# A recurrent attention, a soft and a hard mixture of experts in one launch: the last region's loads, gate logits, constants and order

## Chip, cores and metric

One Trainium2 core runs the whole program as one launch. The metric is device time in microseconds; the kernel before was run three times (median 297.85, from 297.54 to 299.38). All times below are counted from the start of one profiled execution of the kernel before.

## The reference

Three layers in a row, float32, 3072 tokens of 384 features:

1. A gated linear recurrence (4 batches, 8 heads, 768 steps, 48 x 48 states): `S = a*S + k v^T`, `y = q S`, with a complex decay `a`.
2. A soft mixture of experts: `logits = x @ phi` (32 slots, 8 experts of 4); a softmax over tokens mixes the tokens into slots, each expert is `relu(slot @ w1[e]) @ w2[e]` (384 to 1024 to 384), and a softmax over the slots, row by row, mixes slot outputs into tokens.
3. A hard mixture: `logits = x @ w_gate` (8 experts), `e = argmax(logits)`, and each token's output is `gate * (relu(x @ w1[e]) @ w2[e])`, where `gate` is the softmax value of the chosen expert.

The kernel uses that the tokens after layer 2 are mixtures `c @ slot_out` of 32 slots that lie close together. It guesses one expert for all tokens from the mean slot, computes layer 3 for that expert alone, and checks at the end, with flags, that the guess holds for every token; a slow general path stands behind an If.

## The kernel before

`build` writes out three regions, each a list of operations (`Sched`: engine, estimated time, what it reads and writes) and a fixed order for that list, which is stored as an encoded string (`ORDER[0]` to `ORDER[2]`) and applied by `follow`. Each engine executes its own operations in that order; engines wait for one another by semaphores. Where the planner's estimate leaves TensorE a gap, `emit` puts small filler matmuls into the third region (`fill(7)`, line L695; two of them here).

Region 1 (0 to 227 us) is the recurrence. Region 2 (227.6 to 253 us) is layer 2's experts. TensorE streams the weights past 32-column stationary operands (first products L765, second products L794, transposes L774 between them) without a gap. VectorE meanwhile makes the row softmax `cc` from the logits (L847 to L853), its deviation from 1/32 (L880 to L883, which ends in one number per token; TensorE turns it at L885 and broadcasts it at L889), and a threefold copy `c4` of `cc` in the weight buffer `wl[2]` (L860). The region ends with the slot outputs `so4` (L809, ScalarE) and the guessed expert's number `ei` (L822, VectorE).

Region 3 (253 us to the end) is layer 3:

- The mixing weights are turned: for m = 0 to 5, four transposes (L871), a copy to `cS` on ScalarE (L874), and on VectorE a subtraction that replaces one of the three copies by its rounding remainder (L875).
- The gate logits: `so4 @ w_gate` (L898) gives `W2S`, 96 x 8 (split in two by L841 and L842); 24 matmuls with `cS` as the stationary operand and 8 moving columns each (L908) give the logits with tokens on partitions. VectorE takes the maximum (L913) and from it the exponents, the gate and the chosen expert (L914 to L919, L927 to L930); the two matmuls L922 and L925 turn the largest and the smallest choice for the flags.
- The guessed expert's weights: SyncE reads `ei` into a register (L947), then issues two DMAs for the first layer (`m1`, `wl[0]`, 768 KB each, L950) and five for the second (`m2`, `wl[1]`, 384 or 192 KB each, L958). Pieces of `m2` are split into a rounded part `m2h` (L962, ScalarE) and a remainder `m2l` (L964).
- The hidden layer at slot level, in two halves of 512 units: L992 (24 matmuls of 32 x 128), a copy `Gs` (L399) and a square `sq` (L996), transposes by L999 and sums by L1000. VectorE finds the units whose sign is not the same for all tokens (`mixed`, L1006) and numbers them by small matmuls (L1012 to L1016); units that are positive for all tokens (`pos`) enter a linear product, the mixed ones (at most 96) a selection matrix `Pm` (L1021, L1025).
- TensorE accumulates, in one bank, the second layer for the linear and the selected units: `lo` (L1052), `hi` (L1056), `ml` (L1060), two matmuls of 384 columns per piece each, and two float32 products L1044; `Gm` (L1034) collects the selected units' first layer. Results are `W` (split in two, L399 and L1071) and `GmS`.
- The output stage: six products of `GmS` with `cS` (L1079), relu and its remainder (L1080, L1082), and per token tile three matmuls with `W` (L1089, L1090, L1093), scaled by `gate` (L1101, L1102) and written out by 14 DMAs (L1104).

Small constants are made on VectorE at the start of region 3: `okc` (L1110 to L1112, which feed the flag product L1114), unit rows in `GmS` (L983), `trib` and `oneb` (L970, L971), a zero matrix `zr` and zeros in `Pm` (L980, L981).

Of the kernel before, what the change touches and what calls it, by code (L numbers as in the profile page):

```python
# [76 lines left out]
    "6aWAK1ONyC$N<a$&;Zl`*Z|xB-~i+R3;+-S7yu*yTma|*>;N19Gyw1bDF7@0^Z-NvIRHEW_yGI>K>#2CYye~cF#t&bOaM>-XaH~kbO3n(SO9zg2muTM5CIecQ~-<s7y)1akN|)HgaC*DlmM9kpa7%*"  # L77
    "oB*f*tN;K31Oc=FxB$EWzyQPmumBwa",
    "5Ca$h8~_Xhr~n89tN;`P^Z)<=3;+ZG5CH4|@BrWd<N!zj7z0cI=m0DOBmgJ?Gy^aIGyos~2mm|)KmbqxQ~<C5zyK5gEC4tFSO8oAU;tzQ`~Uy}L;z?22mu5EYyc1ebO0Cu3;`SgJOLyD6almVm;fvR"
    "_y9lwNC6-LGyy~bOaUkX!~ie>I04K6Pyx6AlmS!$SOHuCWC6$km;ulLU;&5$XaSr7i~(!`Z~=S)fB|&@paF0I*Z_C|gaOq6qyfDEyaB)gtO2M2+yIaPumQ9I90Pa&oB(_Ppa6sbGy;GCI066y1OmhX"  # L80
    ")Bzv^$N{(k*a6@HqyXFj%mL8><N^2r>;XIiPy+M;2m<i|=>hx!R03E6XaZ~kKmuI?NCI#I6apCnMFLC$3<A&s)B+F!WC9!lAp#@<C<1f>c>>r1d;)<2oC2T%qymfrU;>Z=gaU~I<N_=L=>psWFan4G"
    "i~uA9lmeIn;R2`v`~t87v;wRG$O4c6^a7LsC<E*QFa!7k@dCI4y#fRS00Y1RI0MB3%mM",
# [202 lines left out]
def build(tc, a):  # L285
# [69 lines left out]
    def dma(nbytes, fn, w=(), r=()):  # L355
        op("SP", max(480, nbytes / 340), fn, r=r, w=w, lat=2000)
# [365 lines left out]
    def dma(nbytes, fn, w=(), r=()):  # L722
        op("SP", max(480, nbytes / 360), fn, r=r, w=w, lat=2000)
# [98 lines left out]
    V(8, lambda: vec.tensor_reduce(out=ei[:, 0:1], in_=sp[:, :8], axis=AX.X, op=ALU.max), ["sp"], ["ei"])  # L822
# [8 lines left out]
    W2S = t2("W2S", [128, NE], F32R)  # L831
# [60 lines left out]
    def decl_gate():  # L892
# [6 lines left out]

        M(650, f, ["so4"], [kb_g, "W2S"], kb_g)  # L900

        split(kb_g, W2S, NE, "W2S")
        kb_l = s.bank()

        for m in range(6):
            def f(m=m):
                for u in range(4 * m, 4 * m + 4):
                    pe.matmul(bank(kb_l)[:, NE * u:NE * u + NE], cS[:96, 128 * u:128 * u + 128], W2S[:96], start=True, stop=True)  # L908

            M(430, f, ["W2S", ("cS", m)] + ([kb_l] if m else []), [kb_l] + ([] if m else ["lg"]), None if m else kb_l)  # L910
        lv = lambda: bank(kb_l)[:, :NU * NE].rearrange("p (u e) -> p u e", e=NE)
        b8 = lambda t: t[:, :, None].to_broadcast([128, NU, NE])
        V(192, lambda: vec.tensor_reduce(out=gm, in_=lv(), axis=AX.X, op=ALU.max), [kb_l], ["gm"])  # L913
        V(192, lambda: vec.tensor_tensor(out=eq, in0=lv(), in1=b8(gm), op=ALU.is_equal), [kb_l, "gm"], ["eq"])  # L914
        V(192, lambda: vec.tensor_tensor(out=lg, in0=lv(), in1=b8(gm), op=ALU.subtract), [kb_l, "gm"], ["lg"])
# [11 lines left out]
        A(192, lambda: act(out=lg, in_=lg, func=AF.Exp), ["lg"], ["lg"])  # L927
        V(192, lambda: vec.tensor_reduce(out=gate, in_=lg, axis=AX.X, op=ALU.add), ["lg"], ["gate"])
        V(24, lambda: vec.tensor_scalar(out=gate, in0=gate, scalar1=1e-9, scalar2=None, op0=ALU.add), ["gate"], ["gate"])
        V(200, lambda: vec.reciprocal(out=gate, in_=gate), ["gate"], ["gate"])  # L930

# [14 lines left out]
    m2 = wl[1].rearrange("p (k f) -> p k f", k=8)  # L946
    idx = nc.sync.value_load(ei[0:1, 0:1], min_val=0, max_val=NE)  # L947
    op("SP", 850, lambda: None, w=[("m1", 0)])
    for i in range(2):
        dma(786432, lambda i=i: nc.sync.dma_start(out=m1[:, :, 512 * i:512 * i + 512], in_=a["m2w1"][bass.ds(idx, 1), :, 512 * i:512 * i + 512].rearrange("o (k p) f -> p (o k) f", p=128)),  # L950
            w=[("m1", i)])
# [17 lines left out]
    mixed, trib, oneb = (tf(n, [128, k], BF16) for n, k in (("mixed", 8), ("trib", 128), ("oneb", 128)))  # L969
    V(128, lambda: vec.tensor_copy(out=trib, in_=tri), [], ["trib"], True)  # L970
    V(128, lambda: vec.tensor_copy(out=oneb, in_=ones), [], ["oneb"], True)  # L971
# [4 lines left out]
    GmS = tf("GmS", [96, 128], F32R)  # L976
    W = [tf(f"W{i}", [128, DM], F32R) for i in range(2)]
    zr = tf("zr", [128, 128], F32R)
    kb_gm, kb_a = s.bank(), s.bank()
    V(128, lambda: (vec.tensor_scalar(out=zr, in0=tri, scalar1=0.0, scalar2=None, op0=ALU.mult),  # L980
                    vec.tensor_scalar(out=Pm[:, :, 128:128 + NM], in0=tri[:, None, :NM].to_broadcast([128, 8, NM]), scalar1=0.0, scalar2=None, op0=ALU.mult)), [], ["zr"], True)  # L981
# [391 lines left out]
```

## Time and profile before

| what | value |
|---|---|
| median of three runs | 297.85 us |
| the profiled execution, and its span | 298.1 us, 296.3 us |
| TensorE busy over the span | 275.4 us (93%) |
| region 3 up to the first output matmul | 253.0 to 274.2 us |
| output stage | 274.2 to 288.7 us |
| granted TensorE clock, mean of the span | 0.979 |

Times are microseconds from the start of the execution. A busy TensorE is not TensorE at its peak, since its matmuls are pipelined. The granted clock is a share of 2.4 GHz: 1.00 is 2.4 GHz and 0.50 is 1.2 GHz. A chain of waits lists, in order of time, the pieces of work each of which released the next, back from the last instruction. The 1.8 us between time and span lie outside the recorded instructions.

### The profile page before, as it was taken

Reading aid. Unit: us, or ns where it says so; the run is one execution under the profiler, and the core shown is the slowest. Engines: PE = TensorE matmul, PEld = TensorE weight load, DVE = VectorE, ACT = ScalarE, POOL = GpSimd, SP = SyncE. Lnnn points to the kernel's source line nnn. Section 1 sums busy time; section 2 is a strip of 40 time slices with the busy share of each in tenths; the row PEclk is TensorE's granted clock in tenths of the full one; section 3 lists DMA queues with packets and bytes.
Section 4 is the critical chain, followed back from the end, with each engine's and each line's share of the span. In section 5 each row is a group of like instructions: output and inputs, shape, how many; then the busy total and the mean of one; then the engine's idle time right before and its main releaser. Section 6 shows DMA issues by size and latency. Waiting matters only on the chain.

```text
span 296.3 us, 7880 instructions
## 1 busy us (share of the span) xinstructions
PE 275.4 (93%) x3156; PEld 224.2 (76%) x3156; DVE 239.5 (81%) x493; ACT 228.0 (77%) x429; POOL 117.8 (40%) x81
## 2 busy tenths in 40 slices
PE   0799999999999899999999999999999999899990
PEld 0567688788987798979789898998985344788970
DVE  2579999999999999999999998989647722758850
ACT  3869999999999899999999999987354211525760
POOL 0005657566666756576666736662100000000000
PEclk9999999999999999999999999999999999959996
DMA  6645989834996544342434230199876692380593
GB/s 221 208 135 212 382 297 323 324 80 164 297 376 225 199 137 162 124 143 65 150 88 157 59 105 25 42 329 306 292 263 215 194 376 73 108 319 0 213 327 113
DMA packets 27709, 57.98 MB, mean 196 GB/s; under 512 B 1824, under 2 KB 17568, under 8 KB 27664
## 3 DMA queue, kind: packets, MB, share of 16 engines
q1 hardware_dynamic: 27664, 57.39, 56.4%
q8 instruction: 27, 0.44, 0.6%
q14 instruction: 18, 0.15, 0.2%
HBM read 52.66 MB, written 4.72 MB: 194 GB/s over the span
## 4 chain that ended last, share of the span: by engine, by line
PE 66%; DVE 20%; ACT 6%; issue 3%; DMA 2%; POOL 0%; SPq 0%; POOLq 0%; DVEq 0%
PE bank L526 10%; PE bank L516 10%; PE bank L539 6%; PE bank L543 4%; PE bank L765 4%; PE bank L794 4%; PE bank L457 3%; PE bank L551 3%; PE bank L695 3%; DVE sc L532 2%; PE bank L582 2%; DMA reim<-reim 2%; ACT L697 2%; PE bank L452 2%; PE bank L1089 2%
## 5 line engine op out<-in xcount | busy, mean ns | idle before, releaser
L506 POOL TENSOR_TENSOR kqp<-kqi,lt 128x768 f32<-128x768 f32 x46 | 83.3, 1826 | 59.5 <-ACT lt L427 18.4
L516 PE MATMUL bank<-cst,kqp 128*112 128x128 f32 x384 | 54.0, 276 | 0.0
L526 PE MATMUL bank<-qT,kT 112*128 112x128 f32 x384 | 51.3, 280 | 1.0 <-ACT kT L399 0.4
L526 PEld LDWEIGHTS bank<-qT,kT 112*128 112x128 f32 x384 | 46.4, 191 | 3.5 <-ACT kT L399 1.0
L516 PEld LDWEIGHTS bank<-cst,kqp 128*112 128x112 f32 x384 | 42.0, 133 | 5.8 <-issue 2.2
L697 ACT ACT_TABLE_LOAD x29 | 37.2, 1283 | 1.2 <-PEq L1356 0.7
L539 PE MATMUL bank<-sc,v 128*48 128x128 f32 x384 | 36.8, 277 | 0.0
L532 DVE TENSOR_TENSOR sc<-bank,cst 128x512 f32<-128x512 f32 x48 | 32.8, 686 | 3.1 <-PE bank L526 2.4
L543 PE MATMUL bank<-qT,St 112*48 112x128 f32 x320 | 31.1, 272 | 0.0
L539 PEld LDWEIGHTS bank<-sc,v 128*48 128x48 f32 x384 | 20.2, 122 | 5.9 <-issue 4.2
L419 POOL TENSOR_TENSOR lt<-reim,lt 128x768 f32<-128x768 f32 (+1 forms) x10 | 17.5, 1746 | 12.4 <-ACT lt L418 3.8
L551 PEld LDWEIGHTS bank<-v,kqp 128*48 128x48 f32 x640 | 17.7, 124 | 4.6 <-issue 2.7
L399 ACT COPY qT<-bank 112x512 f32<-112x512 f32 x35 | 20.6, 592 | 0.4 <-PE bank L516 0.4
L695 PE MATMUL bank<-cst 128*48 128x128 f32 x82 | 12.7, 315 | 8.7 <-DMA cst<-cst 8.7
L448 POOL TENSOR_TENSOR hl<-lt,hl 128x384 fp32r<-128x384 f32 x15 | 15.3, 1017 | 13.8 <-ACT hl L446 3.1
L551 PE MATMUL bank<-v,kqp 128*48 128x48 f32 x640 | 20.3, 210 | 0.0
L399 ACT COPY kT<-bank 112x512 f32<-112x512 f32 x30 | 17.2, 587 | 3.6 <-PE bank L516 3.5
L695 PEld LDWEIGHTS bank<-cst 128*48 128x48 f32 x82 | 10.4, 143 | 12.3 <-issue 12.1
L543 PEld LDWEIGHTS bank<-qT,St 112*48 112x48 f32 x320 | 19.1, 123 | 0.0
L399 ACT COPY yT<-bank 112x512 f32<-112x512 f32 x18 | 10.6, 588 | 6.6 <-PE bank L543 6.6
L860 POOL COPY wl<-cc 128x384 f32<-128x384 f32 x1 | 0.7, 659 | 36.3 <-PE bank L794 36.3
L452 PE MATMUL bank<-hl,trir 128*128 128x384 f32 x34 | 14.5, 428 | 0.4 <-DVE acc L651 0.4
(249 smaller groups left out, 626.9 us busy)
## 6 DMA issues: line engine op xcount, KB each, us to landing
wr<-w SPq DMA_DIRECT2D x8, 1536.0 KB, 9.1
kqi<-kq SPq DMA_DIRECT2D x24, 384.0 KB, 3.3
reim<-reim SPq DMA_DIRECT2D x11, 768.0 KB, 4.6
wl<-w SPq DMA_DIRECT2D x5, 1536.0 KB, 7.8
v<-v SPq DMA_DIRECT2D x24, 192.0 KB, 3.7
wr<-w SPq DMA_DIRECT2D x6, 768.0 KB, 8.5
out<-osb SPq DMA_DIRECT2D x10, 384.0 KB, 2.7
wl<-m2w SPq DMA_DIRECT2D x2, 768.0 KB, 5.3
```

The source lines that it names most:

```text
L399: v = {"A": ("ACT", t_act(n, True), lambda: nc.scalar.copy(out=out, in_=in_()), False), "D": ("DVE", t_dve(n), lambda: vec.tensor_copy(out ...
L419: either("P", n, lambda e: e.tensor_tensor(out=l1, in0=im, in1=l0, op=ALU.mult), r=[kim] + k0, w=k1)
L452: pe.matmul(o(), trir, hl[:, 0], start=True, stop=False)
L506: either(e, 768, lambda e, dst=dst, j=j: e.tensor_tensor(out=dst, in0=kq, in1=b(j), op=ALU.mult), r=src + [kj], w=[kd])
L516: pe.transpose(bank(kb)[:112, 128 * i:128 * i + 128], o[:, j, 4 * hf + i], idn)
L526: pe.matmul(bank(kb)[:, 128 * i:128 * i + 128], kTt[ik[hf]][:, i], qTt[iq[hf]][:, i], start=True, stop=True)
L532: op("DVE", t_dve(512), lambda: vec.tensor_tensor(out=sct[ic[hf]], in0=b4(), in1=msk, op=ALU.mult), r=[kb], w=[ksc])
L539: pe.matmul(yps[64 * i:64 * i + 48, pr], v[:, 48 * h:48 * h + 48], sct[ic[hf]][:, h - 4 * hf], start=True, stop=(c == 0))
L543: pe.matmul(yps[64 * i:64 * i + 48, pr], St[:, h], qTt[iq[hf]][:, h - 4 * hf], start=False, stop=True)
L551: pe.matmul(kvps[64 * i:64 * i + 48, h, :48], o[:, 0, h, 64 * i:64 * i + 48], v[:, 48 * h:48 * h + 48], start=True, stop=True)
L695: return lambda: pe.matmul(banks[b][:48, :n], tri[:, :48], idn[:, :n], start=True, stop=True)
L697: tab = lambda t: nc.scalar.preload_act_table_set(TABLES[t])
```

## The change

Line numbers are those of the kernel before unless a line is quoted from the diff.

- Loads: `m2` moves from `wl[1]` to `wl[2]`, where `c4` lies, with its eight blocks rotated by four (`mb`). A piece of `m2` so waits until the transposes that read those blocks of `c4` are done. The first layer's two halves are issued first (second half ahead of the first), then the pieces 0, 4, 2, 1, 3.
- Gate logits: `W2S` becomes a 96 x 224 matrix of zeros with the 8 gate columns at 96 to 103. Six matmuls of 512 columns take windows of it as the stationary operand and `cS` as the moving one; so the logits of block m land on partitions 32(m mod 4) onwards. Two batches (four and two matmuls) each get a copy to SBUF, four transposes and a copy `lg`.
- Constants: `okc`, `trib`, `oneb`, `zr`, the unit rows of `GmS` and the zeros of `W2S` are made in region 2. The zeros in `Pm` are made by one ScalarE instruction at the start of region 3.
- Order: new strings for regions 2 and 3. Read out, region 2's VectorE begins with the constants, the relu of the first half-block is on VectorE ahead of the row sum L850, both `hid` halves are swapped, the turn L885 follows right on the third L765 block, and all of `c4` is on VectorE. In region 3 TensorE runs the flag product L1114, then the transposes 2, 3, 1, 0, the zero product L984, transposes 5, the product L898, transposes 4, the gate logits, the second half of L992, the matmul L925, the first half of L992, the matmul L922, and then the accumulation. Eight fillers stand in four pairs: before and between the logit matmuls, between the logits' transposes, and after the first L992. ScalarE casts `m2h` of piece 0 before it copies `Gs` of the first half; the remainders `m2l` of pieces 0 and 2 are on GpSimd, that of piece 1 on VectorE.

```diff
@@ region 2 and the gate
-    W2S = t2("W2S", [128, NE], F32R)
+    W2S = t2("W2S", [128, 224], F32R)
...
-        split(kb_g, W2S, NE, "W2S")
-        kb_l = s.bank()
-        for m in range(6):
-            def f(m=m):
-                for u in range(4 * m, 4 * m + 4):
-                    pe.matmul(bank(kb_l)[:, NE * u:NE * u + NE], cS[:96, 128 * u:128 * u + 128], W2S[:96], start=True, stop=True)
+        split(kb_g, W2S[:, 96:96 + NE], NE, "W2S")
+        for b, ms in enumerate((range(4), range(4, 6))):
+            kb_t, kb_l, n = s.bank(), s.bank(), 32 * len(ms)
+            def f(ms=ms, kb_t=kb_t):
+                for m in ms:
+                    o = 96 - 32 * (m % 4)
+                    pe.matmul(bank(kb_t), W2S[:96, o:o + 128], cS[:96, 512 * m:512 * m + 512], start=(m == ms[0]), stop=(m == ms[-1]))
+            M(220 * len(ms), f, ["W2S"] + [("cS", m) for m in ms], [kb_t, ("lT", b)], kb_t)
+            copy("A", 512, flat(hT[b], 0)[:n], lambda kb_t=kb_t, n=n: bank(kb_t)[:n], r=[kb_t], w=[("lT", b)])
+            def f(b=b, n=n, kb_l=kb_l):
+                for i in range(4):
+                    pe.transpose(bank(kb_l)[:, n * i:n * i + n], flat(hT[b], 0)[:n, 128 * i:128 * i + 128], idn[:n, :n])
+            M(436, f, [("lT", b)], [kb_l, ("lg", b)], kb_l)
+            copy("A", NE * 4 * len(ms), lg[:, 4 * ms[0]:4 * ms[-1] + 4].rearrange("p (j i) e -> p j i e", i=4),
...
+    okc = t2("okc", [128, NU + 2 * NG])
...
+    trib, oneb = (t2(n, [128, 128], BF16) for n in ("trib", "oneb"))
+    GmS = t2("GmS", [96, 128], F32R)
+    zr = t2("zr", [128, 128], F32R)
...
+    V(216, lambda: (vec.tensor_scalar(out=W2S[:96, :96], in0=tri[:96, :96], scalar1=0.0, scalar2=None, op0=ALU.mult),
+                    vec.tensor_scalar(out=W2S[:96, 96 + NE:], in0=tri[:96, :128 - NE], scalar1=0.0, scalar2=None, op0=ALU.mult))[1], [], ["W2S"])
@@ region 3
-    m2 = wl[1].rearrange("p (k f) -> p k f", k=8)
+    m2 = wl[2].rearrange("p (k f) -> p k f", k=8)
+    def mb(t0, t1):
+        return slice((t0 + 4) % 8, (t0 + 4) % 8 + t1 - t0)
...
-            w=[("m2", k)])
+            w=[("m2", k)] + over)
...
+    op("ACT", t_act(8 * NM), lambda: act(out=Pm[:, :, 128:128 + NM], in_=tri[:, None, :NM].to_broadcast([128, 8, NM]), func=AF.Copy, scale=0.0), w=[("Gp", 0), ("Gp", 1)], tab="E")
```

The rest of the diff changes the planner's estimates, which only the stored order and the number of fillers depend on.

## Rows read from the trace of the kernel before

**Rows 1.** Busy time by stage; after the engines: granted clock, DMA share, GB/s.

```profile
253.00:258.70 5.70, 4.91 (x45) 4.15 (x44) 5.09 (x24) 3.79 (x8) 0.00 (x0) 1.00 0.33 98
258.70:265.80 7.10, 7.07 (x75) 6.15 (x76) 3.62 (x11) 1.18 (x4) 0.00 (x0) 0.60 1.01 367
...
274.30:288.70 14.40, 14.40 (x80) 13.02 (x79) 9.70 (x21) 10.49 (x20) 0.00 (x0) 1.00 0.76 271
```

**Rows 2.** The chain that ended last, 256 to 274 us; columns: start, us, what.

```profile
256.47 1.29 DVE cS L875 x2
...
258.73 2.36 PE bank L908 x16
261.09 1.44 PE bank L992 x24
262.53 0.95 PE bank L908 x4
...
272.24 0.69 PE bank L1060 x4
272.93 0.65 PE bank L1044 x2
```

**Rows 3.** Busy time in half-microsecond stretches, where the granted clock changes.

```profile
260.00:260.50 0.50, 0.50 (x5) 0.50 (x5) 0.49 (x1) 0.00 (x0) 0.00 (x0) 0.60 1.06 414
...
266.50:267.00 0.50, 0.50 (x5) 0.50 (x3) 0.27 (x1) 0.50 (x2) 0.00 (x0) 0.57 0.00 0
```

**Rows 4.** SyncE's DMA issues in order of time, and the landings of line L950.

```profile
255.30 1.04 SPq L950 DMA_DIRECT2D wl<-m2w  x2
...
DMA to landing us min/median/max: 4.6/5.3/6.0
```

**Rows 5.** Instructions in order of time, 253 to 274 us; start, us, what.

```profile
253.24 0.48 ACT L399 COPY so<-bank 128x387 f32<-128x387 f32 x1 [1.10 <-DVE som L808]
...
254.24 0.15 DVE L1112 TENSOR_SCALAR okc<-okt 128x13 f32<-128x13 f32 x1
...
255.66 0.54 DVE L981 TENSOR_SCALAR Pm<-cst 128x768 fp32r<-128x768 f32 x1
...
263.51 0.36 DVE L913 TENSOR_REDUCE gm<-bank 128x24 f32<-128x192 f32 x1 [3.03 <-PE bank L908]
...
265.41 0.42 DVE L1025 TENSOR_TENSOR Pm<-G,pos 128x256 fp32r<-128x256 f32 x1
...
274.18 0.41 PE L1089 MATMUL bank<-W,hh 128*128 128x384 f32 x1
```

**Rows 6.** Instructions in order of time, the row softmax in region 2.

```profile
228.34 0.84 ACT L849 ACTIVATE cc<-cc 128x768 f32<-128x768 f32 x1 [0.82 <-DVE cc L848]
...
229.21 0.95 DVE L850 TENSOR_REDUCE rowm<-cc 128x24 f32<-128x768 f32 x1 [0.91 <-ACT cc L849]
...
234.39 0.18 DVE L883 TENSOR_REDUCE rr<-rowm 128x1 f32<-128x24 f32 x1
```

**Rows 7.** Groups by line, 253 to 274.2 us; busy us, mean ns, idle before.

```profile
L875 DVE TENSOR_TENSOR cS<-bank,cS 32x512 fp32r<-32x512 f32 x6 | 3.8, 682 | 0.1
L874 ACT CAST cS<-bank 96x512 fp32r<-96x512 f32 x6 | 3.2, 585 | 1.5 <-PE bank L871 1.5
...
L962 ACT CAST m2h<-wl 128x768 fp32r<-128x768 f32 x3 | 2.4, 847 | 0.0
```

**Rows 8.** The chain that ended last, in region 2 and in the output stage.

```profile
236.23 0.59 PE bank L774 x4
...
277.53 0.23 PE bank L1079
...
284.58 0.31 PE bank L922 x2
284.89 0.37 PE bank L1089
```

**Rows 9.** The costliest groups of the whole execution (the page), GpSimd's two-input row.

```profile
L506 POOL TENSOR_TENSOR kqp<-kqi,lt 128x768 f32<-128x768 f32 x46 | 83.3, 1826 | 59.5 <-ACT lt L427 18.4
```

More of the change, by code (lines that the diff above doesn't have):

```diff
@@ L911, in decl_gate @@
-        lv = lambda: bank(kb_l)[:, :NU * NE].rearrange("p (u e) -> p u e", e=NE)
+        M(730, f, ["so4"], [kb_g, "W2S"], kb_g)
+        split(kb_g, W2S[:, 96:96 + NE], NE, "W2S")
[12 more added lines that the diff above has]
+            copy("A", NE * 4 * len(ms), lg[:, 4 * ms[0]:4 * ms[-1] + 4].rearrange("p (j i) e -> p j i e", i=4),
+                 lambda ms=ms, kb_l=kb_l: bank(kb_l)[:, :128 * len(ms)].rearrange("p (i j e) -> p j i e", i=4, j=len(ms))[:, :, :, :NE], r=[kb_l], w=[("lg", b)])
@@ L956, in build @@
     for k, (t0, t1) in enumerate(PIECES):
-        h, n = slice(t0, t1), (t1 - t0) * DM
-        dma(196608 * (t1 - t0), lambda h=h, t0=t0, t1=t1: nc.sync.dma_start(out=m2[:, h], in_=a["m2w2"][bass.ds(idx, 1), 128 * t0:128 * t1, :].rearrange("o (k p) f -> p (o k) f", p=128)),
-            w=[("m2", k)])
+        h, hm, n = slice(t0, t1), mb(t0, t1), (t1 - t0) * DM
+        over = [("c4", m) for m in range(hm.start, min(hm.stop, 6))]
+        dma(196608 * (t1 - t0), lambda hm=hm, t0=t0, t1=t1: nc.sync.dma_start(out=m2[:, hm], in_=a["m2w2"][bass.ds(idx, 1), 128 * t0:128 * t1, :].rearrange("o (k p) f -> p (o k) f", p=128)),
+            w=[("m2", k)] + over)
         if t0 >= 8 - NF:
             continue
-        op("ACT", t_act(n), lambda h=h: nc.scalar.copy(out=m2h[:, h], in_=m2[:, h]), r=[("m2", k)], w=[("m2h", k)], tab="E",
-           alt=(("DVE", t_dve(n, True), lambda h=h: vec.tensor_copy(out=m2h[:, h], in_=m2[:, h]), True), ("POOL", t_pool(n), lambda h=h: pool.tensor_copy(out=m2h[:, h], in_=m2[:, h]), True)))
-        either("D" if k % 2 else "P", n, lambda e, h=h: e.tensor_tensor(out=m2l[:, h], in0=m2[:, h], in1=m2h[:, h].bitcast(F32), op=ALU.subtract), r=[("m2", k), ("m2h", k)], w=[("m2l", k)])
+        op("ACT", t_act(n), lambda h=h, hm=hm: nc.scalar.copy(out=m2h[:, h], in_=m2[:, hm]), r=[("m2", k)], w=[("m2h", k)], tab="E",
+           alt=(("DVE", t_dve(n, True), lambda h=h, hm=hm: vec.tensor_copy(out=m2h[:, h], in_=m2[:, hm]), True), ("POOL", t_pool(n), lambda h=h, hm=hm: pool.tensor_copy(out=m2h[:, h], in_=m2[:, hm]), True)))
+        either("D" if k % 2 else "P", n, lambda e, h=h, hm=hm: e.tensor_tensor(out=m2l[:, h], in0=m2[:, hm], in1=m2h[:, h].bitcast(F32), op=ALU.subtract), r=[("m2", k), ("m2h", k)], w=[("m2l", k)])
     Gs, sq = ([tf(f"{n}{i}", [128, 128]) for i in range(2)] for n in ("Gs", "sq"))
@@ L998, in build @@
         o = CST["idn"][0]
-        M(220, lambda i=i, kb2=kb2: pe.matmul(bank(kb2)[:, :132], Gs[i], cst[:, o:o + 132], start=True, stop=True), [("Gs", i)], [kb2, ("G", i)], kb2)
+        M(400, lambda i=i, kb2=kb2: pe.matmul(bank(kb2)[:, :132], Gs[i], cst[:, o:o + 132], start=True, stop=True), [("Gs", i)], [kb2, ("G", i)], kb2)
         M(220, lambda i=i, kb_h=kb_h: pe.matmul(bank(kb_h)[:, :4], sq[i], C("four"), start=True, stop=True), [("sq", i)], [kb_h], kb_h)
@@ L1016, in f @@
                 pe.matmul(o[:, t + 1:], oneb, mixed[:, 4 * i + t:4 * i + t + 1].to_broadcast([128, 3 - t]), start=False, stop=(t == 2))
-        M(120 + 110 * i, f, [("mixed", j) for j in range(i + 1)] + ["trib", "oneb"], [kb_p, ("pf", i)], kb_p)
+        M(280 + 130 * i, f, [("mixed", j) for j in range(i + 1)] + ["trib", "oneb"], [kb_p, ("pf", i)], kb_p)
         V(4, lambda h=h, kb_p=kb_p: vec.tensor_tensor(out=pf[:, h], in0=bank(kb_p)[:, :4], in1=mixed[:, h], op=ALU.mult), [kb_p, ("mixed", i)], [("pf", i)])
         V(128, lambda h=h, gv=gv: vec.tensor_tensor(out=G[:, h, 1], in0=gv(), in1=G[:, h, 0].bitcast(F32), op=ALU.subtract), [kb2, ("G", i)], [("Gl", i)])
-        either("D", 4 * NM, lambda e, h=h: e.tensor_tensor(out=Pm[:, h, :NM], in0=iota[:, None].to_broadcast([128, 4, NM]), in1=pf[:, h, None].to_broadcast([128, 4, NM]), op=ALU.is_equal),
+        either("D", 4 * NM, both=False, fn=lambda e, h=h: e.tensor_tensor(out=Pm[:, h, :NM], in0=iota[:, None].to_broadcast([128, 4, NM]), in1=pf[:, h, None].to_broadcast([128, 4, NM]), op=ALU.is_equal),
                r=[("pf", i)], w=[("Pm", i)])
@@ L1043, in f @@
                 for t in ts:
-                    pe.matmul(bank(kb_a)[:, :DM], PmF[:, t - 8 + NF], m2[:, t], start=False, stop=(t == 7))
+                    pe.matmul(bank(kb_a)[:, :DM], PmF[:, t - 8 + NF], m2[:, mb(t, t + 1).start], start=False, stop=(t == 7))
             M(642 * (t1 - t0), f, ["PmF", "GpF", ("m2", k), kb_a], [("A", k)])
```

63 lines of the change are left out of this document (29 added, 34 removed).

## The prediction

> **What bounds the kernel now.** I read the busy time by stage first [rows 1], to see which engine fills each part of the last region. In the output stage, 274.3 to 288.7 us, TensorE is busy for all 14.40 us; between 258.7 and 265.8 us it is busy too, but at a mean granted clock of 0.60. Second, the chain of waits [rows 2]: behind region 2 it runs through VectorE's remainders L875 until 258.7 us, then through TensorE alone: the logits L908, the first layer's half L992, L908 again, and the accumulation up to L1044. No load stands in it. Third, the clock in half microseconds [rows 3]: it falls to 1.2 GHz inside 260.00 to 260.50 (mean 0.60, so near 260.2) and comes back inside 266.50 to 267.00 (near 266.9). Ahead of the fall TensorE had done transposes and 8-column matmuls; ahead of the rise, two L992 blocks and other wide work. So some 6.7 us of the critical stretch run at half rate.
>
> **The loads: 0.** The two `m1` DMAs start at 255.30 us, the first issue 0.4 to 0.5 us long, and land 4.6 and 6.0 us after their issues [rows 4], so near 259.9 and 261.9 us: in the order of issue, with `m2` queued right behind. L992 began at 261.09, behind L908 [rows 2], not behind a load. Holding `m2` back so makes `m1` no earlier. The new waits for transposes of `c4` (on TensorE the last would end near 257.2 us) queue only the five `m2` issues on SyncE, and until 261.9 us the engines still carry `m1`, so the stream need not break. Were this cover gone, the last piece (near 266 us) would come up to 1 us later; its products stand at the end of the accumulation, after 270 us.
>
> **Constants: the remainders start 1.4 us earlier.** VectorE makes constants from 254.24 us (L1112) [rows 5], and its first L875 starts at 256.47 [rows 2]. Three flag operations of some 0.15 us stay, so VectorE is free at 254.7. It then waits for ScalarE, which ends `so4` at 253.72 [rows 5] and now zeroes `Pm` ahead of the first `cS` copy. ScalarE has no such row; the nearest are 0.84 us for 768 elements on ScalarE (L849) [rows 6] and 0.54 us on VectorE (L981) [rows 5]. I take 0.75 (the first, less the 0.1 by which the next instruction overlaps it) and keep 0.54 to 0.84. With a copy of 0.585 us (L874) [rows 7] the first L875 starts at 255.1. Six of them 0.645 us apart (two take 1.29 [rows 2]) and the split of `W2S` (0.16) end at 259.1; the first four and the split at 257.85. The stall of TensorE for `okc` goes too, worth nothing, since the remainders come later.
>
> **Gate logits: 1.9 us earlier.** Now gm (L913) starts at 263.51 us [rows 5]. New: four 512-column matmuls at 0.23 (L1079) [rows 8] from 257.85 to 258.8, a copy of 0.585; two more after 259.15, so 259.65 with the fillers, a copy to 260.4; transposes at 0.59 per four (L774) [rows 8] with fillers before them, to 261.25; a copy of some 0.3: gm at 261.6. Eight fillers lie in waits, except about 0.25 us ahead of the last transposes.
>
> **The accumulation starts little earlier.** The new order puts L925 on TensorE ahead of the first half of L992. L925 needs gm, three more operations of 0.36 us (L913) [rows 5] with 0.03 between them, and a small one: 261.6 + 4 x 0.39 + 0.2 = 263.35. With its 0.31 us (L922, the same form) [rows 8] the last half of L992 starts at 263.7 and, at full rate, takes half of 1.44 us [rows 2]: 264.45. From the end of such a half to the end of L1025 it is now 265.83 - 262.53 = 3.30 us [rows 2, 5], with 0.95 of L908 between [rows 2], so 2.35. ScalarE adds 0.4: a cast of 0.847 us (L962) [rows 7] is queued ahead of that half's copy and begins only after the gate's exponent, near 264.1. L1025 ends near 267.25. From there TensorE has 16 matmuls at 0.173 (four take 0.69 (L1060) [rows 2]) = 2.75, four float32 products at 0.325 (L1044) [rows 2] = 1.3, L1079 0.23, and eight 96-column matmuls, some 0.6 by the columns of L1060: 4.9 us, to 272.15, and 0.6 to the first output matmul as now (274.18 - 273.58 [rows 2, 5]): 272.8. With its waits between the pieces, 273.0; the same prices on the present order, with its half-rate stretch, give 273.85 where the trace has 274.18 [rows 5], so I add 0.3: **273.3 us, a gain of 0.9.**
>
> The remainders on GpSimd (1.83 us each [rows 9], 0.95 on VectorE at best) begin near 265.3 and end near 267.2 and 269.0; their products stand at about 268.7 and 271.3 on TensorE, so 1.5 us of slack hides them.
>
> **The output stage: a gain of 1.0.** L922 and L925 leave it: each took 0.31 us and made the L1089 behind it 0.37 instead of 0.17 [rows 8]; twice 0.5. They now lie in the gap before the accumulation, where they are counted above. Flags come early; nothing waits for them.
>
> **Region 2: a loss of 0.2.** VectorE makes the constants (about 1.5 us) before and inside the row softmax. More costly is the order: the relu stands ahead of L850, so L850 starts when the first L765 block (ends near 230.3) has had its relu, at 231.1, not 229.21. From L850 to the end of L883 are 234.57 - 229.21 = 5.36 us [rows 6]: 236.45. TensorE reaches the turn L885 at 236.23, when the third block ends (L774) [rows 8]. A stall of 0.2; bounds 0 and 0.6. Should the later reads free the buffers later, the loads L782 have more than 1 us left.
>
> **Sum:** 0.9 + 1.0 - 0.2 = 1.7 us off the profiled execution's 298.1, so 296.4. That execution is 0.25 above the median of 297.85, hence **296.2 us**.
>
> All of it rests on the clock. Priced at full rate throughout, the order of before would reach its first output matmul at 271.4, ahead of the new order's 273.0: the new gate chain is longer, and TensorE's second half waits for it. The gain is the half-rate stretch of before, some 2.4 us, less this. Six wide matmuls and eight fillers between 257 and 262 us are why I expect the clock to hold.
>
> **Rivals.**
>
> - The clock falls where it does now, for as long. For: the 24 transposes L871 stay, and after 261 us there are gaps. The last L992 half costs 0.7 more, the work ahead of it 0.5, the transposes behind it 0.3: 1.5, so **297.7 us**. Chance 0.20.
> - Slower: the clock falls later, at the accumulation. For: between 264.5 and 267 us TensorE has little to do but wait for ScalarE and VectorE, and nothing fills that gap. It decides if the fall comes after about 266: then the 5 us of accumulation and the first output tiles lie in it, and a stretch as long as now (6.7 us) costs half of itself, 3.4: **299.7 us**. Against: TensorE was doing wide work just before. Chance 0.10.
> - Slower too, early: the clock does not count transposes as work and falls before the logit matmuls, near 257, until 264. For: from 253.3 to 257.8 there is hardly anything else (the zero product L984 is one matmul). Against: the same stretch is there now, and the clock stood at 1.00 through 258.7 [rows 1]. Logits, both halves and their transposes would lengthen by 2.2 us: **298.4 us**. Chance 0.06. The Trainium skill says this of transposes ("TensorE: Matmul & The Clock Gate", Part 4: PE-mode transpose): in that mode the full clock does not engage, as it "doesn't count as PE-busy the same way". By that rule the eight added transposes do nothing for the clock either; the row on 253 to 258.7 us does not bear it out.
> - The change doesn't do its first point: the loads were already in order. This is in the forecast, at 0.
> - Better: the accumulation does not wait for the gate chain as priced, and starts as the last `m2` piece lands (near 266). The first output matmul comes at about 271.2, 2 us sooner: **294.2 us**. For: the sum prices VectorE's small operations one after another. Chance 0.14.
>
> **How the numbers follow.** The forecast has a chance of 0.50: 296.2, with bounds 295.4 (no stall in region 2, fewer waits) and 297.0 (0.6 stall, fillers in the way). A measurement tells 1% (3 us: under 294.9, over 300.8) from no change. Only the better case is faster by that much (0.14, and 0.01 from the forecast's edge); slower by that much takes a late fall with a stall on top: 0.03. So faster 0.15, same 0.82, slower 0.03. The range leaves out the best part of the better case and of the late fall: 294.5 to 299.0.
>
> **What would show it.** In the profile after: the first L875 at 255.1 and the last near 258.5; gm near 261.6; a granted clock of 1.00 through 258 to 267; the last L992 half near 263.7, in half of 1.44 us; the first output matmul near 273.3; an output stage of 13.4 us. A load named as releaser of L992 would refute the first part; a half-rate stretch, and where it lies, decides between forecast and rivals.

## The result, and the profile after

The changed kernel is slower: a median of 299.85 us over 20 executions (298.35 to 302.30) against 297.70 for the kernel before in the same comparison (20 executions, 294.90 to 302.27); the ratio is 1.0091, with a 95% interval of 1.0061 to 1.0120. The ratio is within the 1% that the prediction counts as no change, but the median lies above the predicted range (294.5 to 299.0) and on the other side of no change than the forecast of 296.2. The intervals given with ratios leave out executions more than 1.5% above the fastest of their kernel, for the kernel before mostly those in which its clock was low longest, so medians of all executions stand beside them here.

The profiled execution of the changed kernel took 298.99 us, with a span of 297.1. Region 1 ended 2 us sooner in it than in the profiled execution of before, by chance (in the four other profiles of the order of before region 2 starts at 225.01 to 226.32 us), so all points are given from the first matmul of region 2, L765: it starts at 227.57 us in the trace before and at 225.60 after. A time "at 40.4" below is counted from there. The forecast's points are those of the prediction, which counts the 0.2 us of region 2 apart; only the 26.1 has them in it.

| us from the first L765 | before | forecast | after |
|---|---|---|---|
| transposes of `c4` start (L871, now L872) | 25.91 | 26.1 | 26.40 |
| first remainder of `cS` on VectorE (L875, now L876) | 28.90 | 27.5 | 27.78 |
| gm (L913, now L925) | 35.94 | 34.0 | 34.63 |
| last half of the first layer starts (L992, now L1020) | 36.70 | 36.1 | 36.43 |
| `Pm` of the first four tiles done (L1025, now L1053) | 38.26 | 39.7 | 42.88 |
| first output matmul (L1089, now L1117) | 46.61 | 45.7 | 50.45 |
| last output matmul ends | 61.15 | 59.1 | 63.98 |

Up to the last half of the first layer the changed kernel is 0.3 us ahead of before (forecast: 0.6). In the next stage it loses 4 us. Busy time by stage of the changed kernel, answering to [rows 1] (columns: stretch, its length, then busy us of PE, PEld, DVE, ACT and POOL with instructions, the granted clock, the DMA share and GB/s):

```profile
256.70:263.80 7.10, 6.42 (x82) 4.53 (x80) 4.25 (x19) 3.47 (x11) 0.49 (x2) 1.00 1.03 379
265.40:267.70 2.30, 0.02 (x1) 0.02 (x1) 2.23 (x6) 1.10 (x2) 1.88 (x2) 1.00 0.00 0
268.70:272.20 3.50, 3.50 (x14) 3.46 (x15) 2.19 (x7) 0.00 (x0) 0.00 (x0) 0.52 0.00 0
276.05:289.60 13.55, 13.53 (x75) 13.08 (x75) 8.46 (x14) 10.74 (x20) 0.00 (x0) 1.00 0.77 273
```

In the first row, where TensorE ran at 0.60 before, the clock is now 1.00. In the second TensorE does nothing for 2.3 us while VectorE is busy for 2.23 of them in six instructions, and GpSimd for 1.88. In the third TensorE works without a pause, at half rate. The output stage, from the first to the end of the last output matmul, takes 13.53 us instead of 14.54: in the trace before it ends at 288.72.

```profile
288.38 0.34 PE L1093 MATMUL bank<-W,hh 128*128 128x384 f32 x1
```

The clock in half microseconds, answering to [rows 3] (same columns), puts the fall near 268.8 us and the rise near 272.2:

```profile
268.50:269.00 0.50, 0.37 (x2) 0.40 (x3) 0.50 (x3) 0.00 (x0) 0.00 (x0) 0.81 0.00 0
272.00:272.50 0.50, 0.50 (x5) 0.48 (x4) 0.00 (x0) 0.00 (x0) 0.00 (x0) 0.78 0.07 16
```

Its chain of waits, answering to [rows 2] (start, length, what):

```profile
264.25 1.26 DVE fl L1142
...
265.62 1.67 DVE pf L1033
...
267.41 0.23 DVE mixed L1034
...
268.06 0.42 DVE Pm L1053
...
268.63 1.46 PE bank L1080 x4
270.09 0.56 PE bank L1062 x4
```

L1142 handles one element and L1033 four on each partition; such an instruction takes 0.15 us elsewhere in the same trace. Here they take 1.26 and 1.67 us (a hold-up, in what follows), and `Pm` of the first four tiles, which the new order makes last, waits behind them. The timeline of the changed kernel shows what ran beside them (start, length, engine, line, operation, tiles):

```profile
262.30 0.15 DVE L1033 TENSOR_TENSOR pf<-pos 128x4 f32<-128x4 f32 x1
263.67 3.61 POOL L999 TENSOR_TENSOR m2l<-wl,m2h 128x768 fp32r<-128x768 f32 x2
263.78 0.30 DVE L942 RECIPROCAL gate<-gate 128x24 f32<-128x24 f32 x1
264.25 1.26 DVE L1142 SCALAR_TENSOR_TENSOR fl<-sp,e 1x1 f32<-1x1 f32 x1
265.44 0.14 DVE L1031 COPY pos<-bank 128x4 f32<-128x4 f32 x1
265.47 1.81 POOL L999 TENSOR_TENSOR m2l<-wl,m2h 128x768 fp32r<-128x768 f32 x1
265.62 1.67 DVE L1033 TENSOR_TENSOR pf<-pos 128x4 f32<-128x4 f32 x1
267.68 0.16 PE L1040 MATMUL bank<-mixed,trib 128*128 128x4 bf16 x1 [2.33 <-DVE mixed L1034]
```

The two remainders L999 that the new order gave to GpSimd run from 263.67 to 267.28 (the row of two), the second of them from 265.47. L1142 ends at 265.51 and L1033 at 267.29: each ends when a GpSimd instruction does. L1031 between them, which reads PSUM, takes its usual 0.14, and L942, with one operand in SBUF, its usual 0.30. The same L1033 of the other half, before GpSimd started on L999, took 0.15.

The trace of before holds the same event, in region 1, where L461 adds a constant to 384 numbers. Alone it takes 0.34 us; three times GpSimd is at work when it starts, and it takes 0.93, 1.91 and 1.10 us and ends 0.2 us after the GpSimd instruction does. The longest of the three:

```profile
14.43 0.34 DVE L461 TENSOR_SCALAR lt<-lt 1x384 f32<-1x384 f32 x1
...
98.77 1.83 POOL L506 TENSOR_TENSOR kqp<-kqi,lt 128x768 f32<-128x768 f32 x1
98.90 1.91 DVE L461 TENSOR_SCALAR lt<-lt 1x384 f32<-1x384 f32 x1
```

L461 reads one operand, in SBUF, so two operands in SBUF are not the only case.

### The profile page after: what moved, and what is told of

Same layout as the page of the kernel before. It is cut to its first block, busy times and chain, and to the rows that moved or that the text cites. A ratio compares the mean times of both kernels' runs of the same rounds, so it can differ in the third digit from the quotient of the medians.

```text
span 297.1 us, 7895 instructions
## 1 busy us (share of the span) xinstructions
PE 272.7 (92%) x3158; PEld 222.5 (75%) x3158; DVE 240.4 (81%) x495; ACT 229.8 (77%) x432; POOL 120.4 (41%) x82
## 4 chain that ended last, share of the span: by engine, by line
PE 57%; DVE 21%; ACT 5%; issue 3%; POOL 0%; POOLq 0%; DVEq 0%
PE bank L526 9%; PE bank L516 9%; PE bank L539 5%; PE bank L543 4%; PE bank L794 4%; PE bank L551 3%; DVE sc L532 2%; PE bank L582 2%; PE bank L765 2%; PE bank L452 2%; PE bank L453 2%; PE bank L1117 2%; PE bank L1121 1%; PE bank L1118 1%; PE bank L604 1%
## 5 line engine op out<-in xcount | busy, mean ns | idle before, releaser
L526 PEld LDWEIGHTS bank<-qT,kT 112*128 112x128 f32 x384 | 46.4, 191 | 3.4 <-ACT kT L399 1.0
L532 DVE TENSOR_TENSOR sc<-bank,cst 128x512 f32<-128x512 f32 x48 | 32.7, 685 | 3.1 <-PE bank L526 2.4
L1053 POOL TENSOR_TENSOR Pm<-G,pos 128x128 fp32r<-128x128 f32 x1 | 0.4, 400 | 56.4 <-DVE G L1048 56.4
L695 PE MATMUL bank<-cst 128*48 128x128 f32 x94 | 13.7, 298 | 8.8 <-DMA cst<-cst 8.8
```

The lines of the kernel that those rows point to most:

```text
L526: pe.matmul(bank(kb)[:, 128 * i:128 * i + 128], kTt[ik[hf]][:, i], qTt[iq[hf]][:, i], start=True, stop=True)
L532: op("DVE", t_dve(512), lambda: vec.tensor_tensor(out=sct[ic[hf]], in0=b4(), in1=msk, op=ALU.mult), r=[kb], w=[ksc])
L695: return lambda: pe.matmul(banks[b][:48, :n], tri[:, :48], idn[:, :n], start=True, stop=True)
```

## The experiments

Theory A: GpSimd's remainders hold up VectorE instructions that read both operands from SBUF; the last `Pm` is late, TensorE idles, and its clock falls over the accumulation. Rivals: B, the new order is late by itself; C, the clock is the whole loss; D, any VectorE instruction is slowed while GpSimd works; E, the loads matter. Points of the profiled executions, in us from the first L765 (the stretch at half rate up to the last output matmul):

| kernel | first output matmul | stretch at half rate | last output matmul ends |
|---|---|---|---|
| before | 46.61 | 32.5 to 39.4 | 61.15 |
| after | 50.45 | 43.2 to 46.6 | 63.98 |
| e1 remainders on VectorE | 46.28 | none | 59.81 |
| e2 nine fillers | 48.92 | none | 62.45 |
| e3 one SBUF operand | 49.90 | 43.1 to 46.5 | 63.43 |
| e4 loads undone | 51.88 | 42.7 to 49.5 | 65.41 |
| e5 e1, and L886 moved | 46.29 | none | 59.83 |
| e6 before, nine fillers | 49.58 | 35.2 to 45.5 | 64.15 |
| e7 before, one remainder on GpSimd | 52.15 | 32.8 to 46.5 | 66.70 |
| e8 e1 without fillers | 45.67 | none | 59.20 |
| e9 the same kernel | 47.21 | 40.1 to 43.5 | 60.74 |
| e10 e8, flags late | 46.51 | 32.2 to 35.6 | 60.40 |
| e11 before, wide logits | 49.74 | 32.7 to 46.4 | 64.34 |
| e12 e1, flags late | 47.09 | none | 60.62 |
| e13 before, spread fillers | 51.51 | 33.4 to 47.1 | 66.08 |

**e1: the remainders on VectorE.** In the written order `m2l` of the first and third piece go to VectorE, behind that of the second; only those entries of ORDER differ:

```diff
- POOL L999 m2l(0), m2l(2)
+ DVE  L999 m2l(0), m2l(2)    (behind m2l(1); products ml(0) just ahead of ml(2))
```

> The changed kernel with the remainders m2l of pieces 0 and 2 on VectorE, behind that of piece 1, and with piece 0's remainder products just ahead of piece 2's on TensorE; GpSimd keeps only L1053 (128 elements). Measure: from the first L765 to the first output matmul, 50.45 us in the changed kernel, 46.61 before. Theory A (GpSimd's two remainders hold up VectorE's instructions that read two SBUF operands: 1.26 us for a one-element L1142 and 1.67 us for a four-element L1033, and the idle TensorE then loses its clock): both instructions take under 0.25 us, mixed of the first half comes 2.6 us earlier, the clock stays at 1.00 or falls later, and the measure is 46.0 to 47.5; the median falls by 3 to 4 us to about 296. Rival B (the order itself is late: gate chain ahead of the first half, casts ahead of Gs): the two instructions may be short, but VectorE then has 1.8 us more work ahead of the sums, and the measure stays at 49.5 or more.

Timeline of e1:

```profile
264.16 0.15 DVE L1142 SCALAR_TENSOR_TENSOR fl<-sp,e 1x1 f32<-1x1 f32 x1
264.41 0.16 DVE L1033 TENSOR_TENSOR pf<-pos 128x4 f32<-128x4 f32 x1
265.35 0.43 DVE L1053 TENSOR_TENSOR Pm<-G,pos 128x256 fp32r<-128x256 f32 x1
267.02 2.69 DVE L999 TENSOR_TENSOR m2l<-wl,m2h 128x768 fp32r<-128x768 f32 x3
271.78 0.45 PE L1117 MATMUL bank<-W,hh 128*128 128x384 f32 x1
```

```profile
265.40:267.70 2.30, 2.12 (x21) 2.05 (x21) 2.30 (x8) 0.14 (x1) 0.00 (x0) 1.00 0.00 0
268.70:272.20 3.50, 3.39 (x15) 2.38 (x14) 2.95 (x7) 0.99 (x4) 0.00 (x0) 1.00 0.01 2
```

Both small instructions are back at 0.15 and 0.16, TensorE is busy for 2.12 us where it was for 0.02, the clock stays at 1.00, and the first output matmul comes 4.17 us earlier than after. The median of four executions was 296.51 (before, seven executions: 298.71). B falls for the loss against before as profiled: the new order with this one part undone is ahead of it. Against before with its clock held see below.

**e2: nine fillers ahead of the first products with the triangle (L1040).** GpSimd keeps its remainders.

```diff
+    M(213 * 9, lambda: [fill(7)() for _ in range(9)], [], [])   # ahead of L1040
```

> The changed kernel with nine more filler matmuls (about 2 us of TensorE) where TensorE waits for mixed of the first half. Theory A: VectorE's two held-up instructions stay at 1.2 to 1.7 us, the accumulation starts as late as now (43.0 us after the first L765), but the clock does not fall behind it; the half-rate stretch of 3.4 us cost 1.7, so the measure falls from 50.45 to 48.7. Rival C (the clock is all of the loss): the measure falls to 46.6. If fillers do not keep the clock: 50.4.

The clock stays at 1.00 (columns: stretch, length, busy PE, clock, DMA share, GB/s), and the hold-up remains (L1053 ends at 42.9, as in the changed kernel):

```profile
268.50:269.00 0.50, 0.50 (x5) 1.00 0.00 0
```

```profile
265.14 1.70 DVE L1033 TENSOR_TENSOR pf<-pos 128x4 f32<-128x4 f32 x1
274.04 0.44 PE L1117 MATMUL bank<-W,hh 128*128 128x384 f32 x1
```

So the loss splits: 50.45 - 48.92 = 1.53 us is the clock, 48.92 - 46.28 = 2.64 us the hold-up. C falls: with the clock held the change is still 2.3 us behind before.

**e3: one operand from PSUM.** L1033 reads `pos` once from the PSUM bank that it was copied from, and the flags L1142 and L1143 go to the end.

```diff
-    vec.tensor_tensor(out=pf[:, h], in0=pos[:, h], in1=pos[:, h], op=ALU.mult)
+    vec.tensor_tensor(out=pf[:, h], in0=bank(kb2)[:, 128:132], in1=pos[:, h], op=ALU.mult)
```

> The changed kernel with the square L1033 reading one operand from PSUM instead of SBUF, and with L1142 and L1143 at the end of the flags; GpSimd's remainders stay. Theory A (only VectorE instructions with two SBUF operands wait, until the GpSimd instruction ends): L1033 and L1034 are short (under 0.25 us); the wait moves to L1035, the next with two SBUF operands, which takes over 1 us; mixed of the first half comes 2 us earlier, but L1053 and Pm still wait for the second remainder's end, so the measure gains only 0.5 to 1.5 (49 to 50). Rival D (any VectorE instruction is slowed while GpSimd computes): L1033 still takes over 1 us, measure 50.4.

```profile
263.59 3.62 POOL L999 TENSOR_TENSOR m2l<-wl,m2h 128x768 fp32r<-128x768 f32 x2
264.23 0.16 DVE L1033 TENSOR_TENSOR pf<-bank,pos 128x4 f32<-128x4 f32 x1
264.50 0.22 DVE L1034 SCALAR_TENSOR_TENSOR mixed<-bank,rr,pf 128x4 bf16<-128x4 f32 x1
264.75 0.70 DVE L1035 SCALAR_TENSOR_TENSOR pos<-pos,mixed 128x4 f32<-128x4 f32 x1
265.69 1.81 DVE L1053 TENSOR_TENSOR Pm<-G,pos 128x256 fp32r<-128x256 f32 x1
```

With one operand in PSUM, L1033 takes 0.16 us in the middle of GpSimd's work, and so does L1034 its 0.22. The hold-up moves to the next instructions with two SBUF operands: L1035 (0.70 instead of 0.16) ends at 265.45, as GpSimd's first remainder does (half of 3.62 us on, 265.40), L1053 (1.81 instead of 0.43) 0.29 us after the second ends at 267.21. D falls. The time gained is small (0.55 us), since the chain needs those as well and the clock fell here too.

**e4: the loads as before.** `m2` back in its old buffer, without the rotation and the new waits on `c4`.

```diff
-    m2 = wl[2].rearrange("p (k f) -> p k f", k=8)
+    m2 = wl[1].rearrange("p (k f) -> p k f", k=8)
-        over = [("c4", m) for m in range(hm.start, min(hm.stop, 6))]
+        over = []
```

> The changed kernel with the second layer's load back in its own buffer wl[1], unrotated and without the waits for the transposes; all else as changed. Theory A and the prediction: the loads are on no path, the first layer lands in the order of issue: measure 50.45 within 0.4, m1 landings the same. Rival E (the load order matters, by contention or by a held-up queue): a change of over 1 us either way.

L1020 starts its two halves at 34.28 and 36.43, after it was 34.3 and 36.43: the loads move nothing. L1142 and L1033 are held as in the changed kernel (1.27 and 1.67 us). The first output matmul came 1.43 us later, since the clock, which fell at the same place, stayed down for 6.8 us instead of 3.4. That comes without this edit too: of the changed kernel's 20 executions ten have a mean clock of 0.986 or 0.987, as the profiled one (median 298.9 us), and ten 0.982 to 0.984, as e4's 0.984 (median 300.2). E falls; why one low stretch is twice as long as the other isn't settled.

**e5: region 2.** e1 with L886 on TensorE behind the transposes L774 that followed it.

```diff
- PE: L765 (third block), L886, L774, L765 (fourth block)
+ PE: L765 (third block), L774, L886, L765 (fourth block)
```

> The changed kernel with all three remainders of m2 on VectorE (as in e1) and, in region 2, the turn L886 put on TensorE behind the transposes L774 that followed it. Theory A (GpSimd's hold-up of VectorE, and the clock it cost, were the loss; the new order is sound without them): e1 had its first output matmul 46.26 us after the first L765; less the stall of 0.26 us at L886 that is 46.0, against 46.61 in the kernel before, and the output stage stays 0.84 us shorter: 1.4 us less than before from L765 on, a ratio near 0.995. Theory B (the new order is late by itself, e1 was a lucky execution): 46.6 or more after the first L765, ratio 1.00 or over.

The stall of 0.26 us is gone and the fourth block ends 0.46 us sooner, but the second layer then waits for its load, and L805 starts at 24.06 (e1: 24.01):

```profile
245.09 0.11 PEld L794 LDWEIGHTS bank<-wr,hT 128*32 128x32 f32 x2 [0.39 <-DMA wr<-w]
```

The gain of 0.26 was missed. (The output stage is not 0.84 us shorter, as expected, but 1.01.) The median was 295.14 (six executions; before, eleven: 298.30), with a ratio of 0.997, 0.990 to 1.004: unclear.

**e6, e11, e13: the order of before with its clock held.** The prediction priced it at 43.8. e6 puts nine fillers ahead of the first L908; e11 widens each L908 from 8 to 64 columns; e13 spreads eight fillers over the logits and the second half.

```diff
+    M(213 * 9, lambda: [fill(7)() for _ in range(9)], [], [])        # e6, ahead of L908
-    pe.matmul(bank(kb_l)[:, NE * u:NE * u + NE], ..., W2S[:96], ...)  # e11
+    pe.matmul(bank(kb_l)[:, NE * u:NE * u + 64], ..., W2S[:96], ...)
+    M(320 * n, lambda: [fill(7)() for _ in range(n)], [], [])        # e13, at seven places
```

> The kernel before with nine filler matmuls (128 columns, about 0.21 us each) on TensorE ahead of its first logits L908, where it waits for VectorE's remainders. The prediction said that the order of before, at full rate throughout, would reach its first output matmul at 271.4, which is 43.8 us after the first L765. If the half-rate stretch is all that its last region loses, and the fillers keep the clock: 43.8 to 44.3, a ratio near 0.992, and better than every version of the change. If the fillers only move the fall to the gaps behind 262 us: 46.3 to 48, with a granted clock of 0.5 somewhere between 262 and 272 us.

> The kernel before with its 24 logits matmuls L908 widened from 8 to 64 columns (the added columns of W2S are zero, and each is overwritten by the next block); nothing else is changed. If it is the narrow matmuls that make the clock fall there, as e6 (nine fillers ahead of them, and a fall all the same) and e8 (wide logits, no fillers, no fall) suggest: the granted clock stays 1.00 through 258 to 267 us, and the first output matmul comes 43.6 to 44.5 us after the first L765 (the prediction's price of the order of before at full rate was 43.8). If the fall has another cause, such as the transposes or the waits: a stretch of 0.5 again, and 46.3 to 49.6.

> The kernel before with eight fillers spread as the changed kernel has its own: two ahead of the first L908, one ahead of each of the next four, one ahead of the second half's L992 and one ahead of its L999. The changed kernel's stand at 29.9, 31.6, 33.2 and 35.0 us after the first L765, and with them no fall came at 32 us. If it is such spread work that holds the clock there: no stretch of 0.5 between 30 and 40 us, mean clock above 0.99, first output matmul 44 to 45 us after the first L765 (43.8 by the prediction's price of this order at full rate, and some 0.6 for the fillers), and a median near 293.5, since the executions of the kernel before with a mean clock of 0.99 and more had a median of 292.5. If the fall of the kernel before has its cause ahead of the fillers (before 29 us): a stretch of 0.5 from 32 to 35 us on in most runs, and a median of 297 or more.

In all three profiles the clock fell (rows of e6, columns as for e2), and the stretch was longer than in the profile of before:

```profile
260.50:261.00 0.50, 0.50 (x13) 0.60 1.04 366
270.50:271.00 0.50, 0.50 (x4) 0.66 0.00 0
```

e6's median was 299.10 (six executions, ratio 1.009, 1.001 to 1.016), e13's 300.38 (six), e11's one execution 299.99. In two of e13's six executions the clock held (0.992 and 0.993; 296.52 and 293.79 us), in none of e6's. So matmuls of 64 columns did not prevent the fall in e11, and fillers at these places do not do it reliably. The 24 transposes L871 ahead of it stand in all three; they are not ruled out as its cause.

**e7: the hold-up in the kernel before.** One remainder moved to GpSimd.

```diff
- DVE  L964 m2l(0)
+ POOL L964 m2l(0)    (behind its cast)
```

> The kernel before with one remainder, m2l of the first piece (L964), moved from VectorE to GpSimd and issued there as soon as its cast is done, near 267.0 us on the clock of the trace before; the rest of the order as it was. Theory A (GpSimd at work on SBUF holds up VectorE instructions with two SBUF operands until it ends): GpSimd takes 1.8 us, the four-element L1005 of the second half (0.16 us now, at 267.21) ends only when it does, near 268.9, the chain to the second Pm is 1.5 us later, and the first output matmul comes 47.3 to 48.3 us after the first L765 instead of 46.61, although VectorE has 0.91 us less to do. Without a hold-up: L1005 stays at 0.16 us and the first output matmul at 46.6 or up to 0.5 earlier.

```profile
265.19 0.16 DVE L1005 TENSOR_TENSOR pf<-pos 128x4 f32<-128x4 f32 x1
265.65 0.96 DVE L964 TENSOR_TENSOR m2l<-wl,m2h 128x768 fp32r<-128x768 f32 x1
265.80 2.49 POOL L964 TENSOR_TENSOR m2l<-wl,m2h 128x768 fp32r<-128x768 f32 x1 [21.76 <-ACT m2h L962]
266.53 1.78 DVE L1007 SCALAR_TENSOR_TENSOR pos<-pos,mixed 128x4 f32<-128x4 f32 x1
```

L1005 had passed before GpSimd started, so the expectation missed the instruction. It held L1007 instead: 1.78 us against 0.16, until GpSimd ended at 268.29. It works both ways: GpSimd started while VectorE's L964 ran and took 2.49 us, 0.81 of it until that one ended. The time says nothing, since the clock was low from 258.6 to 272.3 us.

**e8, e9, e10, e12: fillers and flags.** e8 is e1 without fillers in the last region, e9 the same kernel timed; e10 is e8 with the flag operations late, e12 is e1 with them late.

```diff
-    s.emit(tab, fill(7), 300, 100)      # e8, e9, e10
+    s.emit(tab, None, 300, 100)
- L1138 ahead of L872; L1139, L1144, L1146, L1141 to L1143 within the gate   # e10, e12
+ L1138 behind L1020; the others ahead of L1145
```

> e1 (the changed kernel with all remainders on VectorE) without any filler matmul in the last region. The prediction gave six wide logit matmuls and eight fillers as the reason why the clock would hold. If the fillers hold it: the granted clock falls to 0.5 between 258 and 266 us and the first output matmul comes 1.5 to 3.4 us later than e1's 46.26 us after the first L765. If the wide matmuls alone hold it: clock 1.00 throughout and 46.0 to 46.3.

> The kernel of e8 again (the changed kernel with all three remainders on VectorE and no fillers in the last region), timed in rounds. Theory A (the hold-up and the clock it cost were the loss; without them the change is a gain, and the fillers only cost their own time): first output matmul 45.7 us after the first L765 against 46.61 before, output stage 0.8 shorter: 1.7 us less than before, a ratio near 0.994. Theory B (the new order is no better): ratio 1.00 or over. If the clock sometimes falls without the fillers, the runs lie in two groups some 1.7 us apart or more.

> e8 with the operations that only make the success flags moved: L1138 on TensorE from ahead of the transposes L872 to behind the first half of L1020, and L1139, L1144, L1146, L1141, L1142 and L1143 on VectorE to the end of the accumulation. If VectorE's short operations lie on the path to the second Pm, as the prediction priced them one after another: L1138 0.18, L1141 0.18 (the wait of L1080), L1142 and L1143 some 0.1: first output matmul 45.2 to 45.4 us after the first L765 (e8: 45.67). If they lie in waits for TensorE and ScalarE: 45.5 to 45.7.

> e1 (the changed kernel with all remainders on VectorE, its fillers kept) with the flag operations moved as in e10. In the profiled executions of e1 and e5 the clock held with the fillers, in 12 executions of the kernel without them it fell in 4, and in e10 it fell at 32.2 us after the first L765. If the fillers hold the clock and the flags lay on the path: mean granted clock 0.992 or more in every run, first output matmul 45.8 to 46.0 us after the first L765 (e1: 46.26), a median 1.0 to 1.3% under that of the kernel before. If the flags lay beside waits: 46.2 to 46.3. If it was L1138's move that brought the fall of e10: a stretch of 0.5 from near 32 us after the first L765, and a mean clock near 0.986 in half of the runs.

e8 seemed to say that the wide logits hold the clock alone. e9, the same kernel, fell:

```profile
265.50:266.00 0.50, 0.44 (x2) 0.82 0.00 0
269.00:269.50 0.50, 0.50 (x4) 0.76 0.00 0
```

Each execution's mean granted clock settles it: without fillers it was under 0.99, as in the profiles with a fall, in 4 of 12 executions (e9; median 295.81, ratio 1.004, 0.999 to 1.010) and 6 of 12 (e10; median 295.23, ratio 1.005, 1.000 to 1.010); with them at 0.990 or more in all 16 of e1, e5 and e12. The flags lead to no gain that can be told: in e10 the clock fell, and in e12 (median 295.01, six executions; before 298.92) the planner put four fillers just ahead of the first output matmul:

```profile
271.18 1.07 PE L695 MATMUL bank<-cst 128*48 128x128 f32 x8
```

**All executions by their clock.** Of the 52 of the kernel before that ran beside e1, e5, e9 and e12, 8 had a mean clock of 0.99 or more (median 292.5 us), 23 between 0.976 and 0.981, as its profiled one (median 297.2), 21 between 0.966 and 0.973 (median 299.7). All 20 of the changed kernel lay between 0.982 and 0.987. The 16 of e1, e5 and e12 have a median of 295.3. So the repaired change is 0.6% below the kernel before as profiled, and 1% above it in the executions in which that one's clock held (five of those eight ran beside e9; beside e1, e5 and e12 there is one each, at 291.53, 293.06 and 292.61). It beats the changed kernel; that it beats the kernel before is likely by the medians and not shown by the interval.

## Why the prediction was wrong, step by step

- **The failed step: "1.5 us of slack hides them".** The remainders on GpSimd were priced by their products alone, at the end of the accumulation. The slack was there: in the changed kernel they end at 41.68 and their products start at 45.62. What they hold up on VectorE was not looked for. From the end of the last L1020 half to the end of L1053 the sum had 264.45 to 267.25, 2.80 us ("2.35" and "ScalarE adds 0.4"). e1 has 262.96 to 265.78, 2.82 us: right. The changed kernel has 263.06 to 268.48, 5.42 us. The Trainium skill states the mechanism ("SBUF — State Buffer", section "Who interferes with whom"): a VectorE instruction with two SBUF inputs and a GpSimd instruction that reads SBUF exclude each other for a whole instruction, and whichever starts first wins. The trace agrees (L1142, L1033, L1035, L1053, L1007 held; L1031, L1034 and L942 not). The trace of before would have priced it, with an instruction of one operand: L461 took 1.91 us instead of 0.34 beside a GpSimd instruction of the remainders' length (1.83 us [rows 9]), and the forecast set two such instructions beside the chain's small operations.
- **The clock.** The forecast was right that it would hold where it fell before: it is 1.00 from 256.7 to 268.5. It was wrong for the whole. The rival with a late fall at the accumulation named the place (the gap between 264.5 and 267 us), the condition (a fall after 266) and, at 299.7, the time. But it priced a low stretch of 6.7 us and no hold-up; in the profile there were 3.4 us of it, worth 1.53, and 2.64 us of hold-up. That its 299.7 (296.2 and 3.4 are 299.6) lies so near the measured 299.85 is luck. With the fillers in place the fall goes with the failed step: by their mean clock it came in all 20 executions of the changed kernel and in none of the 16 without the hold-up, and in e1 TensorE is busy for 1.22 of the 1.60 us from 263.7 on. It is not the only way to a fall there: e9, with neither hold-up nor fillers, fell at 40.1.
- **The fillers as reason.** "Six wide matmuls and eight fillers" is half shown: with the fillers no fall in 16 executions, without them 10 in the 24 of e9 and e10 (in e10 the flags are late as well). As many in the order of before (nine in e6, eight in e13) held it in 2 of 12. What makes the clock fall at 32 to 33 in that order stays open. The prediction took the 1.00 of 253 to 258.7 us as a sign against the transposes L871; the fall came at 260.1, 1.4 us behind that row, so the row does not clear them.
- **The order of before at full rate, 43.8 against 45.7.** No trace shows it. The 8 executions with the clock held are 2.8 us faster than those of the repaired change (292.5 and 295.3), which is the predicted sign; the prediction's terms give 1.9 + 0.2 - 1.0 = 1.1 us. The times of whole executions hold region 1 too, so the size is left open.
- **The loads: 0.** Right (e4).
- **Remainders 1.4 us earlier.** 28.90 became 27.78, 1.1 earlier; of the rest, 0.3 came ahead of the transposes, where L1138 (0.18) now stands. `Pm` on ScalarE took 0.85 us, the 0.84 end of the bound.
- **gm 1.9 us earlier.** It was 1.3, for the same reason and since the chain from the first remainder to gm took 6.85 us instead of 6.5. From gm to the last half of L1020 it took 1.80 instead of 2.1, so that half still started at 36.43 (forecast 36.1). It took 1.02 instead of 0.72; the other half, without L937 among its matmuls, took 0.87.
- **Region 2: 0.2.** Right in size: L805 starts at 24.01 against 23.83. e5 shows a second limit behind it, the load.
- **Output stage: 1.0.** Right: 14.54 became 13.53, 1.01 less.
- **A small slip.** Eight 96-column matmuls at "some 0.6 by the columns of L1060" come to 0.35 by those columns (8 x 96/384 x 0.173); L1034 of before, whose four start some 0.09 apart, gives 0.7, so the 0.6 was near by chance.

With the failed step undone the forecast nearly holds: to the end of the last output matmul it had 1.7 us less than before, and e1 has 1.35 less. Its first output matmul, forecast at 45.73, or 45.9 with the 0.2 us of region 2, came at 46.28. That the median of e1, e5 and e12, 295.3 us, lies 0.9 under the forecast of 296.2 says less, since whole executions hold region 1 too.

## What to carry to other kernels

Moving work to an idle engine is not free because its result is needed late: ask which instructions of its neighbour read SBUF while it runs, with two operands above all, look in the trace for one that was already held up, and price each at up to the whole length of the moved instruction. Here two such hold-ups, of a one-element and of a four-element instruction, idled TensorE and so cost again at its clock. And where a kernel's time depends on whether the clock falls, one profiled execution per version misleads: sort the executions by their mean granted clock before comparing.

## What the runs showed of the hardware

- VectorE instructions of 1 and 4 elements took 0.70 to 1.78 us instead of 0.15 when both operands were in SBUF and a GpSimd instruction of 1.8 us was at work, and ended with it, in two orders of work; with one operand in PSUM they took 0.16 and 0.22 us (e3).
- With one operand in all, in SBUF, one instruction was held up beside GpSimd (L461, 1.91 us instead of 0.34) and another not (L942, 0.30).
- GpSimd waited too: 2.49 instead of 1.8 us when VectorE had started first (e7).
- The low stretches of TensorE's clock, up to the last output matmul, measured 3.4, 6.8, 10.2 and 13.7 us; the same program showed none in one execution and 3.4 us in another (e8, e9).
